# Delta attention with two FFNs: merge products with fp32 operands, the split of T once behind them

## The chip, the cores and the metric

The kernel runs on one core of one Trainium2 chip. The metric is the device time of one execution in microseconds, as the median of several runs. A core has a matrix engine (TensorE, PE in the profile; its weight loads are PEld), a vector engine (VectorE, DVE), a scalar engine (ScalarE, ACT), GpSimd (POOL) and SyncE (SP), which issues the DMAs. They work from the on-chip memory SBUF; TensorE writes its sums to PSUM, from where VectorE and ScalarE fetch them.

## What is computed

A linear attention with the delta rule over 4 batches x 8 heads, 768 positions, head size 48, and on its output two feed-forward networks one after the other (3072 tokens, width 384, hidden 2048). All data are fp32.

```python
k_n = k / (np.linalg.norm(k, axis=-1, keepdims=True) + 1e-06)
for t in range(S):
    y[:, :, t] = np.einsum('bhd,bhde->bhe', q[:, :, t], state)
    v_old = np.einsum('bhde,bhd->bhe', state, kt)
    state = state + bt[:, :, :, None] * np.einsum('bhd,bhe->bhde', kt, vt - v_old)
x = y.transpose(0, 2, 1, 3).reshape(B * S, H * D)
h = x @ w1_in;  x = np.maximum(0.01 * h, h) @ w1_out
h = x @ w2_in;  out = (h - np.tanh(h)) @ w2_out
```

## The kernel before

**Attention in chunks.** The 768 positions are cut into 12 chunks of 64 (n = 0 to 11), two of them to a pair u = 0 to 5. In a chunk the recurrence is replaced by products with a triangular 64x64 matrix T per head: the inverse of one plus the lower triangle of the scaled key gram. A pair has MM = 32 such matrices (2 chunks x NM = 16, with two heads on the upper and lower 64 partitions).

**How T is made.** `grams(n)` multiplies the keys with each other. `g_batch` (line 1035) writes the two diagonal 32x32 blocks of each gram to the room `gd` and the block below the diagonal, split, to `AT`. `inverses(u)` (line 1074) inverts the 32x32 blocks on VectorE, 58 small operations for j = 1 to 30 on all matrices at once, scales the result X, splits it into two fp16 halves Xh, and transposes them once into `nat` (natural order) and once into the second half of `XF`. `merges(u, nat)` (line 1097) then makes the off-diagonal block of T, which is minus one inverse times AT times the other, in two rounds of 32x32 products: the first makes `PM`, the second the block, which goes to `XF`. For u in `M8` (2 to 5) `merges8` does the same with the tiles laid so that eight places of the array are used. `states(n)` multiplies T by the corrected values and keeps the running state; `queries`, `products`, `outputs` make the chunk's output, a tile x of 256 tokens; `to_xa` scales, splits and turns it for the first FFN.

**Precision.** A product of two fp32 operands is made of fp16 ones: each operand is split into a high and a low half (`split`: ScalarE writes the rounded half, VectorE the remainder), and `heads` issues the three products high*high, high*low, low*high into the same sum. A split costs one ScalarE and one VectorE operation.

**FFN.** A token group n has two layers, (n,0) and (n,1), in the order (0,0), (1,0), (0,1), (1,1), (2,0) and so on. A layer has eight steps `h_part` and `o_part`, of groups of 9 or 6 matmuls with full 128x128 weights. The weights are loaded, read from 64-bit words, scaled and split at the start by VectorE and ScalarE (`weight`).

**Rooms.** Tiles come from rings with a number of rooms: `x` (XROOMS; FFN inputs, staging of weights and first keys, at most AMOST = 3 attention outputs at a time), `sx` (SROOMS; scratch), `gd` (one room), `xi` (one room, X).

**What sets the order.** The program is written down as a graph of nodes. `schedule` lays all nodes out with a cost model and one clock per engine: at each point it gives an engine the ready node with the least priority value, which is minus its remaining chain minus an offset from the table `BIAS`, by the node's stage. The resulting order is issued as it is. An operation given with two engines (`cp`) goes to the one that is free. TensorE's small products and FFN groups are issued in turn; `SMALL` holds the cost of one small product by tiling (`quad`), `PAGE` the time that 128 instructions take at least. All matmuls are issued at line 604 and all other operations at line 607, so the profile tells them apart by their tiles.

Of the kernel before, what the change touches and what calls it, by code (L numbers as in the profile page):

```python
# [48 lines left out]
SROOMS = 5  # L49
# [4 lines left out]
    ('consts', 0): -13.87, ('dma', 'b', 0): -307.84, ('dma', 'b', 1): 178.64, ('dma', 'grams', 10): 31.26,  # L54
    ('dma', 'grams', 11): 81.2, ('dma', 'grams', 2): -3.33, ('dma', 'grams', 3): 206.92,
    ('dma', 'grams', 4): 173.01, ('dma', 'grams', 5): 291.69, ('dma', 'grams', 6): 82.58,
    ('dma', 'grams', 7): -8.85, ('dma', 'grams', 8): 154.73, ('dma', 'grams', 9): 159.8,
    ('dma', 'k', 0): 160.49, ('dma', 'k', 1): 57.69, ('dma', 'keys', 10): -43.44, ('dma', 'keys', 11): 40.67,
# [9 lines left out]
    ('dma', 'products', 6): 125.73, ('dma', 'products', 7): -28.88, ('dma', 'products', 8): -7.04,
    ('dma', 'products', 9): 30.32, ('dma', 'queries', 0): 172.91, ('dma', 'queries', 1): 115.5,
    ('dma', 'queries', 10): 41.1, ('dma', 'queries', 11): 122.18, ('dma', 'queries', 2): 73.07,  # L70
    ('dma', 'queries', 3): -96.38, ('dma', 'queries', 4): 119.05, ('dma', 'queries', 5): 26.55,
    ('dma', 'queries', 6): 136.8, ('dma', 'queries', 7): 111.64, ('dma', 'queries', 8): 154.85,
    ('dma', 'queries', 9): 14.63, ('dma', 'to_xa', 1, 1): 130.41, ('dma', 'to_xa', 10, 1): -18.33,
    ('dma', 'to_xa', 11, 1): 29.42, ('dma', 'to_xa', 2, 1): 176.19, ('dma', 'to_xa', 3, 1): -89.32,
    ('dma', 'to_xa', 4, 1): 449.54, ('dma', 'to_xa', 5, 1): 14.05, ('dma', 'to_xa', 6, 1): 131.82,
    ('dma', 'to_xa', 7, 1): 86.81, ('dma', 'to_xa', 8, 1): 25.93, ('dma', 'to_xa', 9, 1): 128.46,
    ('dma', 'v', 0): 204.26, ('dma', 'weight', 0, 0): 102.51, ('dma', 'weight', 0, 1): 117.67,
    ('dma', 'weight', 0, 2): 0.89, ('dma', 'weight', 0, 3): 158.58, ('dma', 'weight', 0, 4): 46.07,
    ('dma', 'weight', 0, 5): -45.97, ('dma', 'weight', 1, 0): 67.45, ('dma', 'weight', 1, 1): 81.55,
    ('dma', 'weight', 1, 2): 53.58, ('dma', 'weight', 1, 3): 102.01, ('dma', 'weight', 1, 4): -5.39,  # L80
    ('dma', 'weight', 1, 5): 203.98, ('dma', 'weight', 2, 0): 114.99, ('dma', 'weight', 2, 1): 178.09,
    ('dma', 'weight', 2, 2): 127.03, ('dma', 'weight', 2, 3): 174.42, ('dma', 'weight', 2, 4): -73.56,
    ('dma', 'weight', 2, 5): 35.14, ('dma', 'weight', 3, 0): 125.81, ('dma', 'weight', 3, 1): 37.25,
    ('dma', 'weight', 3, 2): 113.91, ('dma', 'weight', 3, 3): 83.78, ('dma', 'weight', 3, 4): 355.28,
    ('dma', 'weight', 3, 5): 297.75, ('first_keys', 0): -39.35, ('grams', 0): 40.8, ('grams', 0, 1): 22.94,
    ('grams', 1): 38.75, ('grams', 1, 1): -39.7, ('grams', 10, 1): 144.33, ('grams', 11, 1): -20.86,
    ('grams', 2, 1): 51.08, ('grams', 3, 1): -75.12, ('grams', 4, 1): 7.24, ('grams', 5, 1): -0.11,
    ('grams', 6, 1): 173.8, ('grams', 7, 1): 4.91, ('grams', 8, 1): 56.4, ('grams', 9, 1): 20.21,
# [7 lines left out]
    ('inverses', 2, 1): -24.61, ('inverses', 3): -36.01, ('inverses', 3, 1): 11.53, ('inverses', 4): -32.07,
    ('inverses', 4, 1): 105.6, ('inverses', 5): 257.21, ('inverses', 5, 1): -51.28, ('keys', 10): -0.31,
    ('keys', 11): -76.39, ('keys', 2): 38.41, ('keys', 3): -12.4, ('keys', 4): -4.68, ('keys', 5): -349.49,
    ('keys', 6): 50.02, ('keys', 7): -41.11, ('keys', 8): 56.89, ('keys', 9): -8.53, ('merges', 0): 66.31,
    ('merges', 2): 165.98, ('merges', 3): 90.69, ('merges', 4): 190.95, ('merges', 5): 51.66,  # L100
# [6 lines left out]
    ('outputs', 10, 1): 37.88, ('outputs', 11, 1): 38.21, ('outputs', 2, 1): 2.77, ('outputs', 3, 1): 93.97,  # L107
    ('outputs', 4, 1): 141.64, ('outputs', 5, 1): -19.0, ('outputs', 6, 1): 8.74, ('outputs', 7, 1): 128.81,
    ('outputs', 8, 1): 206.17, ('outputs', 9, 1): 5.82, ('products', 0): 23.33, ('products', 1): 19.0,
    ('products', 10): 133.22, ('products', 11): 15.61, ('products', 2): 189.16, ('products', 3): 165.45,  # L110
    ('products', 4): -13.34, ('products', 5): -8.58, ('products', 6): -3.82, ('products', 7): -1.91,
    ('products', 8): 29.1, ('products', 9): -10.35, ('queries', 0): 287.56, ('queries', 1): -40.81,
    ('queries', 10): -12.87, ('queries', 11): 81.5, ('queries', 2): 13.89, ('queries', 3): -13.13,
    ('queries', 4): 153.28, ('queries', 5): -16.43, ('queries', 6): 35.77, ('queries', 7): 157.84,
    ('queries', 8): 9.36, ('queries', 9): 55.72, ('states', 0): -10.01, ('states', 0, 1): 0.39,
    ('states', 0, 2): -161.78, ('states', 1): 73.59, ('states', 1, 1): 17.21, ('states', 1, 2): 21.55,
    ('states', 10): -7.11, ('states', 10, 1): 9.72, ('states', 10, 2): 6.87, ('states', 11): -174.19,
    ('states', 11, 1): -16.97, ('states', 2): -23.01, ('states', 2, 1): 118.94, ('states', 2, 2): -9.83,
    ('states', 3): 31.95, ('states', 3, 1): -7.84, ('states', 3, 2): 17.01, ('states', 4): 37.67,
    ('states', 4, 1): 104.03, ('states', 4, 2): -34.7, ('states', 5): 76.0, ('states', 5, 1): 119.15,  # L120
    ('states', 5, 2): -13.08, ('states', 6): 8.7, ('states', 6, 1): 80.62, ('states', 6, 2): 83.82,
# [1449 lines left out]
```

## Time and profile before

| | us |
|---|---|
| median of 3 runs (990.19 to 990.79) | 990.56 |
| profiled execution | 990.11 |
| its span in the trace | 988.4 |
| TensorE busy | 875.9 (89%) |
| VectorE busy | 723.5 (73%) |
| ScalarE busy | 594.7 (60%) |

Busy shares are means over stages with different limits, so they are read by stages: first in the 40 slices of the page, then in the table of stretches. Matmuls overlap in the array: the duration of one is longer than the distance to the next, and a group's cost is read from the start of one group to the start of the next. The granted TensorE clock is 0.999 of full speed over the span.

### The profile page before, as it was taken

How to read it: one execution, taken by the hardware profiler on the slowest of the kernel's cores; microseconds unless marked ns; L12 is line 12 of the kernel's file. 1: busy time of each engine (PE TensorE's matmuls, PEld its weight loads, DVE VectorE, ACT ScalarE, POOL GpSimd, SP SyncE). 2: the span in 40 equal slices, each digit the busy share in tenths (PEclk: the TensorE clock that was granted, in tenths of full speed). 3: DMA queues.
4: the chain of work that ended last, by engine and by line, in shares of the span. 5: the costliest groups of instructions: out<-in, count | busy, mean ns of one | idle time of the engine just before them, and what ended most of it. 6: DMA issues, size and time to landing. Idle time of an engine off the chain costs nothing.

```text
span 988.4 us, 37304 instructions
## 1 busy us (share of the span) xinstructions
PE 875.9 (89%) x16680; PEld 719.4 (73%) x16680; DVE 723.5 (73%) x1714; ACT 594.7 (60%) x1324; POOL 5.9 (1%) x21
## 2 busy tenths in 40 slices
PE   1102399999999999999999999999999999999997
PEld 1102378887788887788877788887788878788875
DVE  7999999999799764699576896764479647342432
ACT  6949865777886864476866545852554545434431
POOL 2000000000000000000000000000000000000000
PEclk9999999999999999999999999999999999999999
DMA  9952544320524000331002300110110001010000
GB/s 354 398 161 65 164 150 135 112 83 26 125 78 93 4 18 18 60 92 43 19 19 62 77 19 19 46 40 18 38 31 18 3 1 40 18 35 1 2 17 17
DMA packets 69280, 67.11 MB, mean 68 GB/s; under 512 B 42752, under 2 KB 54016, under 8 KB 69120
## 3 DMA queue, kind: packets, MB, share of 16 engines
q1 hardware_dynamic: 69120, 64.74, 23.3%
q8 instruction: 130, 2.13, 0.9%
q14 instruction: 30, 0.25, 0.1%
HBM read 44.14 MB, written 4.72 MB: 49 GB/s over the span
## 4 chain that ended last, share of the span: by engine, by line
PE 73%; DVE 13%; ACT 8%; DMA 3%; issue 2%; SPq 0%; ACTq 0%; DVEq 0%
PE ps_h L604 34%; PE ps_o L604 32%; PE ps_a L604 7%; ACT sx L607 2%; DVE wi L607 2%; ACT jk L607 2%; DVE xi L607 2%; DVE wo L607 2%; DVE sx L607 2%; ACT XF L607 1%; DMA kf<-in_k_dram 1%; DVE gd L607 1%; DVE g L607 1%; DVE pq L607 1%; ACT gd L607 1%
## 5 line engine op out<-in xcount | busy, mean ns | idle before, releaser
L604 PE MATMUL ps_h<-x,wi 128*128 128x256 f16 x3456 | 408.9, 274 | 0.8 <-DVE sx L607 0.5
L604 PEld LDWEIGHTS <-wi 128*128 128x128 f16 x3456 | 334.7, 98 | 49.4 <-issue 2.6
L604 PE MATMUL ps_o<-g,wo 128*128 128x256 f16 x1728 | 204.8, 273 | 0.1
L604 PE MATMUL ps_o<-wo,g 128*128 128x384 f16 x1152 | 200.7, 326 | 0.4 <-ACT sx L607 0.4
L604 PEld LDWEIGHTS <-wo 128*128 128x128 f16 x1728 | 166.7, 98 | 19.6
L607 ACT ACTIVATE g<-sx 128x512 f16<-128x512 f32 x192 | 120.3, 627 | 90.4 <-DVE sx L607 51.7
L604 PEld LDWEIGHTS <-g 128*128 128x128 f16 x1152 | 110.7, 98 | 66.8 <-issue 0.9
L607 DVE SCALAR_TENSOR_TENSOR sx<-sx,kap,ps_h 128x512 f32<-128x512 f32 x96 | 71.4, 744 | 65.3 <-ACT sx L607 65.1
L607 ACT ACTIVATE sx<-ps_h,kap 128x512 f32<-128x512 f32 x96 | 65.1, 679 | 65.7 <-PE ps_h L604 50.8
L607 DVE TENSOR_TENSOR g<-sx,g 128x512 f16<-128x512 f32 x96 | 65.8, 686 | 47.0 <-ACT g L607 46.4
L607 DVE SCALAR_TENSOR_TENSOR g<-sx,g 128x512 f16<-128x512 f32 x96 | 66.2, 689 | 45.7 <-ACT g L607 45.4
L607 ACT ACTIVATE sx<-ps_h 128x512 f32<-128x512 f32 x96 | 56.9, 592 | 68.9 <-PE ps_h L604 48.6
L607 DVE TENSOR_TENSOR gd<-xi 128x30 f32<-128x30 f32 (+9 forms) x180 | 58.8, 327 | 2.2
L607 DVE TENSOR_TENSOR xi<-xi,gd 128x30 f32<-128x30 f32 (+9 forms) x180 | 59.0, 328 | 2.0
L604 PEld LDWEIGHTS <-ones 128*128 128x128 bf16 x124 | 8.0, 100 | 59.3 <-issue 45.1
L604 PEld LDWEIGHTS <-KTp 48*64 48x64 f16 x3360 | 34.3, 114 | 19.9 <-issue 19.3
L607 ACT ACTIVATE jk<-kf 128x48 bf16<-128x48 f32 x160 | 38.4, 240 | 4.3 <-DMA kf<-in_k_dram 0.9
L604 PE MATMUL ps_a<-ab,ones 128*128 128x1 bf16 x60 | 7.9, 166 | 29.4 <-ACT sx L607 23.8
L607 ACT ACTIVATE sx<-x 128x768 bf16<-128x768 f32 x24 | 20.2, 843 | 20.0 <-DVE x L607 19.6
L607 DVE SCALAR_TENSOR_TENSOR XF<-ps_a,XF 32x256 f16<-32x256 f32 (+1 forms) x40 | 19.9, 497 | 15.2 <-ACT XF L607 14.2
L607 ACT ACTIVATION_READ_ACCUMULATOR jk<-kf 128x1 f32 x160 | 30.1, 188 | 0.0
L607 DVE SCALAR_TENSOR_TENSOR wi<-wo,wi 128x768 int32<-128x768 int32 x32 | 29.7, 948 | 0.0
(138 smaller groups left out, 983.0 us busy)
## 6 DMA issues: line engine op xcount, KB each, us to landing
wo<-in_w_in_dram SPq DMA_DIRECT2D x32, 384.0 KB, 7.9
qf<-in_q_dram SPq DMA_DIRECT2D x24, 256.0 KB, 2.9
wi<-in_w_out_dram SPq DMA_DIRECT2D x14, 384.0 KB, 8.0
kf<-in_k_dram SPq DMA_DIRECT2D x12, 384.0 KB, 4.1
vf<-in_v_dram SPq DMA_DIRECT2D x12, 384.0 KB, 3.5
out_dram<-sx SPq DMA_DIRECT2D x48, 96.0 KB, 2.2
x<-in_w_out_dram SPq DMA_DIRECT2D x10, 384.0 KB, 5.6
b<-in_beta_dram SPq DMA_DIRECT2D x6, 512.0 KB, 4.0
```

The source lines that it names most:

```text
L604: self.eng["pe"].matmul(out=o.real(), lhsT=lhsT.real(), rhs=rhs.real(), start=start, stop=stop)
L607: getattr(self.eng[n.on], op)(**{k: v.real() if isinstance(v, View) else v for k, v in kw.items()})
```

## The change

The 32x32 products of both merge rounds take fp32 operands: one product in place of three fp16 ones. What they read is no longer split: `AT` and `PM` are fp32 tiles, each written by one copy, and the inverse's result is transposed as fp32. The transposed X in natural order goes to the room of `gd` and not to that of X. T is split at the end of `merges`, once per chunk of the pair: ScalarE copies to a new tile `XH`, and VectorE writes the remainder to `XF`. `states` reads the high half from `XH`. `gd` has two rooms, `x` four in place of six, `sx` six in place of five. The two forms of the merge are one function. The planner counts an fp32 product as two instructions and has two more costs in `SMALL`. All offsets in `BIAS` have other values.

```diff
-XROOMS = 6
+XROOMS = 4
...
-SROOMS = 5
+SROOMS = 6
...
-    SMALL = ((0.0163, 0.028), (0.0094, 0.0139), (0.0065, 0.0139))
+    SMALL = ((0.0163, 0.028), (0.0094, 0.0139), (0.0065, 0.0139), (0.027, 0.045), (0.017, 0.03))
...
+        node.cnt += 1 + (lhsT.ap.dtype == F32)
...
-    gd_r = ring("gd", 1, MM * HB)
+    gd_r = ring("gd", 2, MM * HB)
...
-    AT = fixed("AT", [128, 2, NM, 2 * HB], F16)
-    PM = fixed("PM", [128, 2, NM, HB], F16)
+    AT = fixed("AT", [128, NM, 2 * HB], F32)
+    PM = fixed("PM", [128, NM, HB], F32)
     XF = fixed("XF", [128, MM, C, 2], F16)
+    XH = fixed("XH", [128, MM, C], F16)
...
-            split(AT[:, 0, av], AT[:, 1, av], ps.rearrange("p (m a) n -> p m (a n)", a=2)[:, :, HB:HB + C], 1.0 / KS)
+            cp(AT[:, av], ps.rearrange("p (m a) n -> p m (a n)", a=2)[:, :, HB:HB + C], 1.0 / KS)
...
-        Xh = Gd.rearrange("p m j -> p (m j)").bitcast(F16).rearrange("p (i j c) -> p i j c", i=HB, c=2)
-        nat = X.rearrange("p m j -> p (m j)").bitcast(F16).rearrange("p (m j c) -> p m j c", m=MM, c=2)
-        copy(Xh[:, :, :, 0], X)
-        tt(Xh[:, :, :, 1], X, Xh[:, :, :, 0], ALU.subtract)
-        transpose(packed(nat).rearrange("p m j -> p j m"), packed(Xh).rearrange("p i j -> p j i"))
-        transpose(XW[:, :, HB:].rearrange("p m i -> p i m"), packed(Xh))
+        nat = Gd
+        transpose(nat.rearrange("p m j -> p j m"), X.rearrange("p i j -> p j i"))
+        transpose(XW[:, :, HB:].rearrange("p m i -> p i m"), X)
...
+        def rounds(jobs):
+            ps = banks(HB)
+            for m in range(GM):
+                for f, h in HF:
+                    jobs(ps[f], m, m + f * GM, HQ[2 * h], HQ[2 * h + 1], *spots(f, h))
+            return ps
+
+        def first(ps, m, i, up, dn, out_up, out_dn):
+            mm(ps[out_dn, m], AT[up, i, 0:HB], nat[up, 2 * i])
+            mm(ps[out_up, m], AT[dn, i, HB:], tt_[dn, 2 * i + 1])
+
+        def second(ps, m, i, up, dn, out_up, out_dn):
+            mm(ps[out_up, m], PM[dn, i], tt_[dn, 2 * i])
+            mm(ps[out_dn, m], nat[up, 2 * i + 1], PM[up, i])
+
+        ps = rounds(first)
+        for f in range(2):
+            fm = slice(f * GM, (f + 1) * GM)
+            if f and eight:
+                for h in range(2):
+                    cp(PM[HS[h], fm], ps[f][HS[1 - h]], 1.0 / KS)
+            else:
+                cp(PM[:, fm], ps[f], 1.0 / KS)
+        ps = rounds(second)
...
+                    cp(xm[HQ[2 * h], a][:, f * GM:(f + 1) * GM], ps[f][spots(f, h)[a]], -1.0 / KS)
+        for s in range(2):
+            g_.stage = "merges", u, s
+            ms = slice(s * NM, (s + 1) * NM)
+            copy(XH[:, ms], XW[:, ms])
+            tt(XF[:, ms, :, 0], XW[:, ms], XH[:, ms], ALU.subtract)
...
-                heads([(ps[g][HS[h ^ g], m], [XF[HS[h], m0 + g * GM + m, :, c_] for c_ in range(2)],
+                heads([(ps[g][HS[h ^ g], m], [XH[HS[h], m0 + g * GM + m], XF[HS[h], m0 + g * GM + m, :, 0]],
```

## Rows read from the trace of the kernel before

**Rows 1.** The page: shares by engine, and TensorE's busy tenths in 40 slices

```profile
PE 875.9 (89%) x16680; PEld 719.4 (73%) x16680; DVE 723.5 (73%) x1714; ACT 594.7 (60%) x1324; POOL 5.9 (1%) x21
...
PE   1102399999999999999999999999999999999997
```

**Rows 2.** Table by stages: stretch, length, busy us of PE, PEld, DVE, ACT, POOL

```profile
0.00:100.00 100.00, 14.70 (x905) 12.81 (x906) 92.66 (x236) 72.81 (x239) 5.87 (x21) 1.00 0.69 244
100.00:125.00 25.00, 8.63 (x444) 7.87 (x428) 24.07 (x38) 21.43 (x41) 0.00 (x0) 1.00 0.58 168
...
200.00:250.00 50.00, 50.00 (x1125) 39.50 (x1123) 49.13 (x109) 37.43 (x62) 0.00 (x0) 1.00 0.21 63
250.00:300.00 50.00, 49.49 (x1290) 38.58 (x1279) 44.95 (x130) 40.50 (x127) 0.00 (x0) 1.00 0.42 101
...
950.00:988.00 38.00, 33.27 (x253) 24.41 (x250) 12.31 (x18) 11.15 (x18) 0.00 (x0) 0.99 0.09 22
```

**Rows 3.** Order of time, TensorE: start us, duration us, instruction group, count

```profile
245.97 1.15 PE L604 MATMUL ps_h<-x,wi 128*128 128x256 f16 x9
246.96 1.14 PE L604 MATMUL ps_o<-wo,g 128*128 128x384 f16 x6
```

**Rows 4.** Order of time, TensorE, around one merge round

```profile
478.33 2.13 PE L604 MATMUL ps_h<-x,wi 128*128 128x256 f16 x18
480.38 0.18 PE L604 MATMUL ps_a<-XF,PM 32*32 32x32 f16 x1
...
481.92 0.18 PE L604 MATMUL ps_a<-PM,xi 32*32 32x32 f16 x1
482.04 2.69 PE L604 MATMUL ps_o<-g,wo 128*128 128x256 f16 x23
```

**Rows 5.** Table by stages, only instructions on PM: TensorE, weight loads, VectorE, ScalarE

```profile
85.00:130.00 45.00, 1.90 (x192) 1.67 (x96) 0.69 (x1) 0.57 (x1) 1.00 0.44 134
...
465.00:485.00 20.00, 1.72 (x192) 1.59 (x96) 1.27 (x3) 1.14 (x3) 1.00 0.10 32
```

**Rows 6.** Costliest groups by form, VectorE, then ScalarE: count, busy us, mean ns

```profile
L607 DVE SCALAR_TENSOR_TENSOR XF<-ps_a,XF 32x256 f16<-32x256 f32 x32 | 14.1, 440 | 14.5 <-ACT XF L607 13.7
...
L607 DVE SCALAR_TENSOR_TENSOR AT<-ps_a,AT 128x256 f16<-128x256 f32 x24 | 9.9, 417 | 0.3 <-ACT AT L607 0.2
...
L607 DVE TENSOR_TENSOR gd<-xi,gd 128x1024 f16<-128x1024 f32 x6 | 8.2, 1360 | 2.1 <-ACT gd L607 2.0
...
L607 DVE SCALAR_TENSOR_TENSOR XF<-ps_a,XF 32x512 f16<-32x512 f32 x8 | 5.8, 722 | 0.7 <-ACT XF L607 0.6
...
L607 ACT ACTIVATE XF<-ps_a 32x256 f16<-32x256 f32 x32 | 14.4, 449 | 10.2 <-PE ps_a L604 8.0 <-DVE XF L607 1.4
...
L607 ACT ACTIVATE AT<-ps_a 128x256 f16<-128x256 f32 x24 | 8.7, 382 | 1.3 <-DVE gd L607 1.2
L607 ACT ACTIVATE gd<-xi 128x1024 f16<-128x1024 f32 x6 | 8.1, 1348 | 1.7 <-DVE xi L607 1.7
...
L607 ACT ACTIVATE PM<-ps_a 128x256 f16<-128x256 f32 x4 | 1.5, 384 | 0.1
```

**Rows 7.** Order of time, VectorE and ScalarE, around the first merge

```profile
80.74 0.19 DVE L607 TENSOR_SCALAR xi<-b 128x32 f32<-128x32 f32 x1
...
84.83 2.06 DVE L607 STREAM_TRANSPOSE xi<-gd 128x1024 f32<-128x1024 f32 x1
...
103.10 0.71 ACT L607 ACTIVATE XF<-ps_a 32x512 f16<-32x512 f32 x1
...
110.42 0.73 DVE L607 SCALAR_TENSOR_TENSOR XF<-ps_a,XF 32x512 f16<-32x512 f32 x1
```

**Rows 8.** Order of time, TensorE: the first FFN group

```profile
129.13 5.33 PE L604 MATMUL ps_h<-x,wi 128*128 128x256 f16 x27
```

**Rows 9.** Order of time: the third group's turning DMAs, and its first FFN products

```profile
267.58 3.06 SPq L607 DMA_TRANSPOSE x<-sx  x2
...
274.42 1.16 PE L604 MATMUL ps_h<-x,wi 128*128 128x256 f16 x9
```

More of the change, by code (lines that the diff above doesn't have):

```diff
@@ L53 @@
 BIAS = {
[L54 to L58, printed above, removed]
@@ L68 @@
[L68 to L73, printed above, removed]
@@ L74 @@
[L74 to L88, printed above, removed]
[6 rows of a table removed]
-    ('inverses', 0, 1): 133.5, ('inverses', 1): -36.38, ('inverses', 1, 1): 15.22, ('inverses', 2): 14.02,
@@ L96 @@
[L96 to L100, printed above, removed]
[6 rows of a table removed]
@@ L107 @@
[L107 to L121, printed above, removed]
@@ L137 @@
-    ('weight', 2, 3): 129.61, ('weight', 2, 4): -141.25, ('weight', 2, 5): -344.98, ('weight', 3): 225.17,
-    ('weight', 3, 0): -12.03, ('weight', 3, 1): -38.44, ('weight', 3, 2): 187.06, ('weight', 3, 3): -214.7,
-    ('weight', 3, 4): -52.05, ('weight', 3, 5): -64.53,
+    ('consts', 0): 44.43, ('dma', 'b', 0): -17.81, ('dma', 'b', 1): -51.45, ('dma', 'grams', 10): -22.99,
+    ('dma', 'grams', 11): -129.47, ('dma', 'grams', 2): -0.05, ('dma', 'grams', 3): 125.77,
+    ('dma', 'grams', 4): -19.78, ('dma', 'grams', 5): 12.19, ('dma', 'grams', 6): 1.87,
@@ new lines @@
+    ('dma', 'grams', 7): 35.25, ('dma', 'grams', 8): 31.51, ('dma', 'grams', 9): -132.02,
+    ('dma', 'k', 0): 296.83, ('dma', 'k', 1): 143.48, ('dma', 'keys', 10): -31.98, ('dma', 'keys', 11): -101.3,
+    ('dma', 'keys', 2): -110.92, ('dma', 'keys', 3): 52.43, ('dma', 'keys', 4): -15.95,
+    ('dma', 'keys', 5): -130.9, ('dma', 'keys', 6): 92.75, ('dma', 'keys', 7): -8.09, ('dma', 'keys', 8): 1.78,
+    ('dma', 'keys', 9): 8.74, ('dma', 'o_part1', 0): -21.77, ('dma', 'o_part1', 1): 2.63,
[3 rows of a table added]
+    ('dma', 'o_part1', 9): 0.54, ('dma', 'products', 1): -1.65, ('dma', 'products', 10): -65.54,
@@ new lines @@
+    ('dma', 'products', 11): -88.37, ('dma', 'products', 2): 27.28, ('dma', 'products', 3): 18.26,
+    ('dma', 'products', 4): -65.22, ('dma', 'products', 5): 40.06, ('dma', 'products', 6): 64.27,
+    ('dma', 'products', 7): -62.2, ('dma', 'products', 8): -4.58, ('dma', 'products', 9): -255.86,
+    ('dma', 'queries', 0): 84.04, ('dma', 'queries', 1): -7.71, ('dma', 'queries', 10): -17.82,
+    ('dma', 'queries', 11): -69.89, ('dma', 'queries', 2): -186.5, ('dma', 'queries', 3): 3.67,
+    ('dma', 'queries', 4): -29.26, ('dma', 'queries', 5): 34.02, ('dma', 'queries', 6): 174.44,
@@ new lines @@
+    ('dma', 'queries', 7): -27.52, ('dma', 'queries', 8): -38.4, ('dma', 'queries', 9): -6.15,
+    ('dma', 'to_xa', 1, 1): -42.59, ('dma', 'to_xa', 10, 1): 22.52, ('dma', 'to_xa', 11, 1): 48.23,
+    ('dma', 'to_xa', 2, 1): 26.16, ('dma', 'to_xa', 3, 1): -478.07, ('dma', 'to_xa', 4, 1): 1.83,
+    ('dma', 'to_xa', 5, 1): 237.5, ('dma', 'to_xa', 6, 1): 35.5, ('dma', 'to_xa', 7, 1): -16.95,
+    ('dma', 'to_xa', 8, 1): 51.23, ('dma', 'to_xa', 9, 1): 3.9, ('dma', 'v', 0): 225.47,
+    ('dma', 'weight', 0, 0): -27.26, ('dma', 'weight', 0, 1): -156.01, ('dma', 'weight', 0, 2): -11.99,
@@ new lines @@
+    ('dma', 'weight', 0, 3): 1.29, ('dma', 'weight', 0, 4): -89.97, ('dma', 'weight', 0, 5): -86.75,
+    ('dma', 'weight', 1, 0): -23.46, ('dma', 'weight', 1, 1): 5.49, ('dma', 'weight', 1, 2): 50.54,
+    ('dma', 'weight', 1, 3): 10.62, ('dma', 'weight', 1, 4): -20.79, ('dma', 'weight', 1, 5): -31.76,
+    ('dma', 'weight', 2, 0): -56.23, ('dma', 'weight', 2, 1): 143.18, ('dma', 'weight', 2, 2): 8.17,
+    ('dma', 'weight', 2, 3): 214.07, ('dma', 'weight', 2, 4): -20.18, ('dma', 'weight', 2, 5): 226.33,
@@ new lines @@
+    ('dma', 'weight', 3, 0): 128.96, ('dma', 'weight', 3, 1): 187.1, ('dma', 'weight', 3, 2): -31.75,
+    ('dma', 'weight', 3, 3): -26.07, ('dma', 'weight', 3, 4): 51.88, ('dma', 'weight', 3, 5): -38.04,
+    ('first_keys', 0): 57.64, ('grams', 0): -24.9, ('grams', 0, 1): 125.6, ('grams', 1): 115.12,
+    ('grams', 1, 1): 1.43, ('grams', 10, 1): -13.77, ('grams', 11, 1): 22.01, ('grams', 2, 1): 108.23,
+    ('grams', 3, 1): 39.17, ('grams', 4, 1): 5.07, ('grams', 5, 1): 5.39, ('grams', 6, 1): 11.59,
@@ new lines @@
+    ('grams', 7, 1): 51.09, ('grams', 8, 1): 374.08, ('grams', 9, 1): 184.06, ('h_part0', 1): -13.01,
[5 rows of a table added]
+    ('h_part1', 9): 90.06, ('inverses', 0): 273.98, ('inverses', 0, 1): 131.38, ('inverses', 1): -6.39,
+    ('inverses', 1, 1): -109.27, ('inverses', 2): -211.61, ('inverses', 2, 1): -3.41, ('inverses', 3): -28.95,
+    ('inverses', 3, 1): -5.18, ('inverses', 4): 3.56, ('inverses', 4, 1): -104.28, ('inverses', 5): -95.8,
+    ('inverses', 5, 1): 102.63, ('keys', 10): 61.37, ('keys', 11): 23.57, ('keys', 2): 122.59,
@@ new lines @@
+    ('keys', 3): -6.83, ('keys', 4): -11.38, ('keys', 5): -13.92, ('keys', 7): 24.96, ('keys', 8): -37.52,
+    ('keys', 9): -120.64, ('merges', 0, 0): 126.87, ('merges', 0, 1): -43.4, ('merges', 1): 5.6,
+    ('merges', 1, 0): 1.89, ('merges', 1, 1): -51.37, ('merges', 2): 39.99, ('merges', 2, 0): 20.13,
+    ('merges', 2, 1): 23.04, ('merges', 3): 784.36, ('merges', 3, 0): 2.83, ('merges', 3, 1): 47.44,
+    ('merges', 4): 26.05, ('merges', 4, 0): 0.64, ('merges', 4, 1): 18.95, ('merges', 5): 17.46,
[7 rows of a table added]
@@ new lines @@
+    ('outputs', 10, 1): 20.55, ('outputs', 11, 1): 59.41, ('outputs', 2, 1): 66.82, ('outputs', 3, 1): 345.83,
+    ('outputs', 4, 1): 183.51, ('outputs', 5, 1): 2.83, ('outputs', 6, 1): 33.99, ('outputs', 7, 1): 47.99,
+    ('outputs', 8, 1): -13.85, ('outputs', 9, 1): -39.8, ('products', 0): 125.94, ('products', 1): 28.97,
+    ('products', 10): 21.01, ('products', 11): -64.74, ('products', 2): -90.46, ('products', 3): -17.53,
+    ('products', 4): 117.48, ('products', 5): -18.97, ('products', 6): 202.39, ('products', 7): 5.4,
@@ new lines @@
+    ('products', 8): -29.14, ('products', 9): -56.63, ('queries', 0): -6.34, ('queries', 1): 172.78,
+    ('queries', 10): 3.07, ('queries', 11): -21.08, ('queries', 2): -7.18, ('queries', 3): 139.78,
+    ('queries', 4): -38.97, ('queries', 5): -5.89, ('queries', 6): 77.76, ('queries', 7): 7.73,
+    ('queries', 8): 11.86, ('queries', 9): -130.03, ('states', 0): 117.73, ('states', 0, 1): 1.16,
+    ('states', 0, 2): 118.21, ('states', 1): 29.8, ('states', 1, 1): 127.32, ('states', 1, 2): 222.14,
@@ new lines @@
+    ('states', 10): 85.47, ('states', 10, 1): -38.5, ('states', 10, 2): 0.5, ('states', 11): 2.26,
+    ('states', 11, 1): 47.85, ('states', 2): 21.61, ('states', 2, 1): 275.33, ('states', 2, 2): -13.21,
+    ('states', 3): -63.86, ('states', 3, 1): 59.1, ('states', 3, 2): -80.7, ('states', 4): -30.61,
+    ('states', 4, 1): 24.82, ('states', 4, 2): 261.68, ('states', 5): 91.41, ('states', 5, 1): -3.9,
+    ('states', 5, 2): -118.03, ('states', 6): 6.89, ('states', 6, 1): 109.91, ('states', 6, 2): 12.47,
@@ new lines @@
+    ('states', 7): 28.51, ('states', 7, 1): 4.1, ('states', 7, 2): -1.55, ('states', 8): 129.07,
+    ('states', 8, 1): 96.12, ('states', 8, 2): -5.11, ('states', 9): 0.64, ('states', 9, 1): 136.26,
+    ('states', 9, 2): -103.01, ('to_xa', 0): 63.34, ('to_xa', 0, 1): 73.9, ('to_xa', 1): 14.69,
+    ('to_xa', 10): 9.0, ('to_xa', 2): 40.2, ('to_xa', 3): -15.21, ('to_xa', 4): -3.44, ('to_xa', 5): 82.58,
+    ('to_xa', 6): 95.59, ('to_xa', 7): 45.37, ('to_xa', 8): -3.58, ('to_xa', 9): -1.28, ('to_xb', 0): 29.67,
@@ new lines @@
+    ('v_scale', 9): 11.54, ('weight', 0): 8.04, ('weight', 0, 0): 5.8, ('weight', 0, 1): 245.24,
+    ('weight', 0, 2): 60.75, ('weight', 0, 3): -2.78, ('weight', 0, 4): 49.61, ('weight', 0, 5): 5.35,
+    ('weight', 1): 60.34, ('weight', 1, 0): 2.29, ('weight', 1, 1): 277.75, ('weight', 1, 2): 16.46,
+    ('weight', 1, 3): 38.15, ('weight', 1, 4): -13.11, ('weight', 1, 5): 52.14, ('weight', 2): 155.89,
+    ('weight', 2, 0): -61.34, ('weight', 2, 1): 12.16, ('weight', 2, 2): -6.18, ('weight', 2, 3): 86.59,
@@ L140 @@
+    ('weight', 2, 4): 201.91, ('weight', 2, 5): 9.67, ('weight', 3): -4.9, ('weight', 3, 0): 234.55,
+    ('weight', 3, 1): 127.64, ('weight', 3, 2): 37.63, ('weight', 3, 3): 0.46, ('weight', 3, 4): 7.5,
+    ('weight', 3, 5): -39.32,
 }
@@ L345, in matmul @@
             self.open.warm = self.open.cold = 0.0
-            self.open.mode = 0
+            self.open.mode = self.open.cnt = 0
             self.open.stage = self.stage
@@ L511, in schedule @@
             if e == "pe" and n.mode:
[L512 removed]
+                c = n.cnt
                 at = t + (n.warm * left_on / c if c >= left_on else n.warm + (left_on - c) * 0.109)
@@ L1098, in merges @@
         g_.stage = "merges", u
-        def two(t, r, m):
-            return [t[r, m, :, c_] for c_ in range(2)]
-        tt_ = XF[:, :, HB:]
-        def bank2():
-            t = g_.tile(ps_a, [128, 512], F32)
-            g_.cut()
-            return t.rearrange("p (m n) -> p m n", m=NM)
-        xm = tt_.rearrange("p (m a) i c -> p a m i c", a=2)
-        if u in M8:
-            merges8(u, nat, two, tt_, xm)
-            return
-        ps = bank2()
-        for m in range(NM):
-            if m == GM:
-                g_.cut()
-            jobs = []
-            for h in range(2):
-                up, dn = HQ[2 * h], HQ[2 * h + 1]
-                jobs += [(ps[dn, m], [AT[up, c_, m, 0:HB] for c_ in range(2)], two(nat, up, 2 * m)),
-                         (ps[up, m], [AT[dn, c_, m, HB:] for c_ in range(2)], two(tt_, dn, 2 * m + 1))]
-            heads(jobs)
@@ L1124, in merges @@
-        split(PM[:, 0], PM[:, 1], ps, 1.0 / KS)
-        ps = bank2()
-        for m in range(NM):
-            if m == GM:
-                g_.cut()
-            jobs = []
-            for h in range(2):
-                up, dn = HQ[2 * h], HQ[2 * h + 1]
-                jobs += [(ps[up, m], parts(PM, dn, m), two(tt_, dn, 2 * m)),
-                         (ps[dn, m], two(nat, up, 2 * m + 1), parts(PM, up, m))]
-            heads(jobs)
-        for a in range(2):
-            for h in range(2):
-                o = xm[HQ[2 * h], a]
-                split(o[:, :, :, 0], o[:, :, :, 1], ps[HQ[2 * h + a]], -1.0 / KS)
@@ new lines, in merges, with spots @@
+        tt_ = XW[:, :, HB:]
+        eight = u in M8
+        HF = [(f, h) for f in range(2) for h in range(2)]
+        g_.quad = 4 if eight else 3
+        def spots(f, h):
+            w = h ^ f if eight else h
+            return HQ[2 * w], HQ[2 * w + 1]
+        def rounds(jobs):
[7 more added lines that the diff above has]
+            mm(ps[out_up, m], AT[dn, i, HB:], tt_[dn, 2 * i + 1])
@@ L1167, in merges8 @@
         g_.quad = True
+        xm = tt_.rearrange("p (m a) i -> p a m i", a=2)
         for f in range(2):
@@ L1247, in states @@
                 for m in range(GM):
-                    heads([(ps[HS[h], m], [XF[HS[h], m0 + g * GM + m, :, c_] for c_ in range(2)],
+                    heads([(ps[HS[h], m], [XH[HS[h], m0 + g * GM + m], XF[HS[h], m0 + g * GM + m, :, 0]],
                             parts(R[:, g], HS[h], m)) for h in range(2)])
```

60 lines of the change are left out of this document (8 added, 52 removed), and 30 rows, old and new, of the table BIAS.

## The prediction, on record before the changed kernel was run

> **What bounds the kernel now.** I read the page's shares first, then the table by stages, then the order of time on TensorE. TensorE is busy 89% of a span of 988.4 us, and its slices show why it is not more: four slices almost empty, then nines to the end [rows 1]. By stages [rows 2] the first 100 us hold 14.70 us of TensorE work, while VectorE is busy 92.66; in 100 to 125 VectorE has 24.07 of 25. From there TensorE is the full one: 50.00 of 50 in 200 to 250, 49.49 in 250 to 300. The last stretch, 33.27 of 38, holds the final scaling and store. The FFN begins at 129.13 [rows 8]. So the time is a start of 129 us that VectorE and one chain set, and after it a TensorE that goes from one FFN group to the next, with the attention's small products put between them. What the change takes off TensorE after 129 us comes off the time one for one, as long as each FFN layer finds its input. What it takes off VectorE counts only up to the first layers: VectorE is still busy 49.13 of 50 in 200 to 250 and 44.95 in the next 50 [rows 2], and the input of the third token group is turned by DMAs issued at 267.58 and first used at 274.42 [rows 9]. The run-up to that use is nearly as tight as the start.
>
> **The price of a small product.** A merge of one chunk pair u has two rounds of 192 products with 32x32 operands in fp16 [rows 5]. The order of time shows a whole round: it begins at 480.38, its last product starts at 481.92 and the FFN goes on at 482.04 [rows 4]. That is 1.66 us, of which 1.54 go to 191 steps: 8.1 ns per product, and some 0.12 us for leaving the mode. An FFN group of nine products with 256 columns takes 0.99 us from its start to the next group's [rows 3], 110 ns per product or 0.43 ns per column; 32 columns at that rate are 13.8 ns. So the small products already overlap in the array, and what I see is a rate of instructions. After the start there are five merges, ten rounds, at 1.66 us: 16.6 us.
>
> **Part 1: fp32 products instead of three fp16 ones.** 64 products per round take the place of 192. No row shows an fp32 product. The diff counts each as two instructions, and that decides my value: two at the measured rate of 8.1 ns are 16.2 ns, 64 of them 1.04 us, with entering and leaving 1.2 us. The low end is one instruction's price: 64 x 8.1 ns + 0.12 = 0.64 us. The high end is an fp32 product that goes through four times and overlaps with none: 4 x 13.8 = 55 ns, a round of 3.5 us. I take 1.2, because the operands and output tiles lie in the same places as in the overlapping rounds. Ten rounds then give 12.0 instead of 16.6 us: **-4.6 us**, with ends -10 and +19.
>
> The Trainium skill (FP8 and Floating Point Precision, "TensorE Precision Notes") says that a true fp32 product takes four passes through the array. No run here shows one. By four passes at the instruction price a round is 64 x 4 x 8.1 ns = 2.07, with 0.12 it is 2.2 us: ten rounds cost 22, or 5.3 us more than now. It stands below as a rival.
>
> **Part 2: the start.** For the first merge the steps lie on the chain to the first FFN product.
> - The inverse's last step is at 80.74, done at 80.93; the transposes begin at 84.83 [rows 7]. In between lies the split of X that the change deletes: 1.36 us on ScalarE and 1.33 on VectorE here, with weight work between. The transposes read X itself now. Gain up to 3.9 us; if weight work fills the place, only VectorE's own 1.3.
> - The first round's result was split in 0.57 + 0.69 us, one behind the other [rows 5]. Now two halves are copied, 0.38 each [rows 6], on either engine at once: -0.7 to -0.9.
> - The second round's result was split from 103.10 to 111.15 (110.42 + 0.73) [rows 7], 8.0 us, of which four pairs with 0.72 each are 5.8 [rows 6]. Now eight copies at 0.44 to 0.45 over two engines are 1.8 us, and then come the copy to XH and the subtraction for the first half, 1024 elements each, 1.35 and 1.36 by the rows of the old split with the same size [rows 6]: 4.5 us. With the 2.2 us of foreign work that lay between, 6.7: -1.3.
> - First and second round on TensorE: 64 against 192 products; at 1.2 for 1.66 us, -0.5 each at the same rate.
> Together -3.9 - 0.8 - 1.3 - 1.0 = -7.0 for the chain by itself. But VectorE was full in those stretches, and what is pulled forward pushes weight conversion back, which the second FFN layers need. VectorE's own account for the first two merges limits the gain: before, 1.36 + 0.69 + 4 x 0.72 + 4 x 0.42 (the split of AT) = 6.6 us each; after, two subtractions of 1.36 and a half of the fourteen copies (4 AT, 2 PM, 8 XF, together 5.9) = 5.7, or 2.7 if ScalarE, which has 72.8 of 100 us in use at the start [rows 2], takes them all. So VectorE is relieved by 1 to 4 us per merge, 2 to 8 over both. I take **-5 us** for the first FFN product, and the same for the third group's input. Ends: -8, and +3 if the two new steps at the end (2.7 us) stand on the chain while the place of the old split fills with other work.
>
> **Part 3: what moves without a price.** Later merges save more vector work (eight pairs of 0.44 become eight copies, the AT split halves), but no engine except TensorE is full after 300 us: nothing. The states' products read the upper part from XH and the lower from XF; same count, same shape: nothing. The second gram room lets the next chunk pair's grams be written while the inverse, which now keeps its result in that room, is still being read. Without it the next grams would wait for the second merge round; with it nothing waits. Two x rooms fewer: a token group's input and the second layer's input hold a room for one layer each, and three attention inputs at most are admitted as before, so four rooms hold a pair and the next pair; the two that staged weights are free again before the third group. If that is wrong the price shows at the third group, whose use follows the turning by only 274.42 - 267.58 = 6.8 us, most of it the DMAs. One more scratch room can only admit work earlier. New offsets put every step at another place; the single idle pieces in the stages after 150 are some tenths of a microsecond (0.51 in 250 to 300 [rows 2]), so an order as dense as this gains no more than 2 us, and a worse one may cost as much: 0, +-2.
>
> **Sum.** Against the profiled execution (990.11 us: span 988.4 and 1.7 around it): 990.1 - 4.6 - 5 = 980.5. The median of the runs, 990.56, is 0.45 above, so the prediction is **981 us**.
>
> **Rivals.**
> *The start gives its gain back.* VectorE was the full engine until 250 us; the FFN begins earlier, but the second weights or the third group's input come as late as before, and TensorE idles for the difference. For it: 49.13 of 50 in 200 to 250. Against it: VectorE loses work too. Then only Part 1 counts: 990.6 - 4.6 = 986.
> *Four times the price, by the rule above.* +5.3 on ten rounds, -5 from the start: about 991, no change. Against it: two instructions per product in the diff. For it: the row's rate was only seen with fp16.
> *fp32 products do not overlap (slower).* Place: the ten rounds after 129 us and the two before. Price: 3.5 + 0.12 against 1.66 us, +2.0 each, +20; the start's -5 becomes about -1 since its two rounds are longer by 4. Time: 990.6 + 20 - 1 = 1009. Break-even is where ten rounds cost 16.6 + 5 us: 2.16 us each, less 0.12, 32 ns per product. From there on it is slower. Against it: the fp16 rounds overlap with the same tiles.
>
> The Trainium skill (TensorEngine Tiling (Array Packing), "Instruction Overhead") gives each matmul an overhead of about 60 cycles, 25 ns at 2.4 GHz. The round of 192 in 1.66 us says 8.1 ns; as a rate the rule does not hold here. By it, 64 instructions fewer per round would be -16 us over ten rounds instead of -4.6, and I give it no weight.
>
> **How the numbers follow.** Chances: forecast 0.52, start given back 0.15, four times the price 0.13, no overlap 0.10, and 0.10 that the new order is worse than the old by more than it saves (a wait for a room or for the third group; 993 to 1000). Faster by over 0.2% (about what a measurement of this kernel can tell from no change, 2 us) are the first two: 0.67; within it 0.13; slower 0.20. The range leaves out 2 in 10, half of it at each end: below, merges at 0.8 us per round (-8.6) and a start of -8 give 974; above, it takes in the no-change case and the beginning of the worse orders: 995.
>
> **What would show it.** Right: TensorE's matmul records fall by 2304 fp16 and rise by 1536 (two per fp32 product); a round takes 1.1 to 1.3 us from its first product to the next FFN group; transposes start within 1 us of the inverse's last step; the first FFN product is at 124, the third group's input as much earlier. Wrong: rounds over 2.1 us, a first FFN product after 129, or TensorE idle in 150 to 300 that before was not there.

## The result

The changed kernel takes 978.86 us (median of four runs, 977.31 to 981.46) against 990.67 for the kernel before: a ratio of 0.9884, 95% interval 0.9863 to 0.9906. It is 1.2% faster, 11.8 us; the prediction said 981. The profiled execution took 978.71 us with a span of 977.0, 11.4 less than before.

The page of the changed kernel shows the same picture as [rows 1], with 768 matmul records fewer (15912 for 16680):

```profile
PE 872.3 (89%) x15912; PEld 716.6 (73%) x15912; DVE 700.9 (72%) x1653; ACT 584.2 (60%) x1329; POOL 5.9 (1%) x21
...
PE   2201499999999999999999999999999999999997
```

The stages of [rows 2] after the change (stretch, length, busy us of PE, PEld, DVE, ACT, POOL, then granted clock, DMA share, GB/s). VectorE is about as full as before up to 200 us (92.34 for 92.66 in the first 100) and a little less in 200 to 250 (46.87 for 49.13), where TensorE now stands 2.4 us:

```profile
0.00:100.00 100.00, 17.92 (x889) 15.28 (x893) 92.34 (x233) 66.20 (x180) 5.87 (x21) 1.00 0.69 238
100.00:125.00 25.00, 11.41 (x527) 10.07 (x520) 25.00 (x42) 20.95 (x44) 0.00 (x0) 1.00 0.62 174
...
200.00:250.00 50.00, 47.63 (x967) 36.97 (x965) 46.87 (x119) 35.08 (x66) 0.00 (x0) 1.00 0.28 67
250.00:300.00 50.00, 49.79 (x1193) 39.23 (x1192) 46.04 (x119) 37.29 (x119) 0.00 (x0) 1.00 0.36 87
```

A merge round in the order of time on TensorE, to be held against [rows 4], and one of the four groups of fp32 products:

```profile
333.98 0.21 PE L608 MATMUL ps_a<-XF,PM 32*32 32x32 f32 x1
...
335.07 0.19 PE L608 MATMUL ps_a<-PM,gd 32*32 32x32 f32 x1
335.20 0.50 PE L608 MATMUL ps_o<-g,wo 128*128 128x256 f16 x3
...
L608 PE MATMUL ps_a<-PM,gd 32*32 32x32 f32 x384 | 8.6, 205 | 0.0
```

The round takes 335.20 - 333.98 = 1.22 us. Four groups of 384 records are 1536 for 768 products: an fp32 product is two matmul records in the trace. The first FFN product, the third group's turning DMAs and its first products, against [rows 8, 9]:

```profile
124.53 3.41 PE L608 MATMUL ps_h<-x,wi 128*128 128x256 f16 x18
...
264.43 2.57 SPq L611 DMA_TRANSPOSE x<-sx  x2
...
270.40 3.11 PE L608 MATMUL ps_h<-x,wi 128*128 128x256 f16 x27
```

**Where the 11.4 us of the span went.** The FFN begins 4.6 us earlier (129.13 to 124.53). From there to the end it takes 852.5 in place of 859.3 us, 6.8 less. The ten rounds are 3.7 of that: nine of 1.22 and one of 2.04, in which TensorE stood, 0.6 us of it in one wait; 13.0 for 16.8. The other 3.0 us are spread: adding up from each matmul's start to the next one's, FFN products take 764.5 us for 767.0, the chunks' other small products 65.5 for 67.4 (one group of 96 moved ahead of the first FFN product), and the sums over partitions 4.0 for 2.7, with a wait of 1.4 for VectorE behind one of them, until 246.21.

### The profile page after: what moved, and what is told of

It reads as the page before. It is cut to its first block, busy times and chain, and to the rows that moved or that the text cites. A ratio compares the mean times of both kernels' runs of the same rounds, so it can differ in the third digit from the quotient of the medians.

```text
span 977.0 us, 35741 instructions
## 1 busy us (share of the span) xinstructions
PE 872.3 (89%) x15912; PEld 716.6 (73%) x15912; DVE 700.9 (72%) x1653; ACT 584.2 (60%) x1329; POOL 5.9 (1%) x21
## 4 chain that ended last, share of the span: by engine, by line
PE 83%; DVE 8%; DMA 4%; ACT 3%; issue 1%; SPq 1%; ACTq 0%; DVEq 0%
PE ps_o L608 38%; PE ps_h L608 37%; PE ps_a L608 8%; DVE wi L611 2%; DVE wo L611 2%; DMA wi<-in_w_out_dram 1%; ACT jk L611 1%; DMA wo<-in_w_in_dram 1%; DVE sx L611 1%; DMA kf<-in_k_dram 1%; DMA qf<-in_q_dram 1%; ACT sx L611 1%; DVE gd L611 1%; DVE XF L611 1%; SPq L611 1%
## 5 line engine op out<-in xcount | busy, mean ns | idle before, releaser
L608 PE MATMUL ps_h<-x,wi 128*128 128x256 f16 x3456 | 403.1, 273 | 2.3 <-DVE sx L611 1.7
L608 PE MATMUL ps_o<-g,wo 128*128 128x256 f16 x1728 | 200.0, 273 | 0.3 <-issue 0.2
L608 PE MATMUL ps_a<-wacc,ones 128*128 128x1 bf16 x64 | 2.7, 165 | 34.7 <-ACT wi L611 24.6
L611 DVE TENSOR_SCALAR p<-ps_a 128x1 f32<-128x1 f32 x40 | 6.2, 154 | 37.1 <-PE ps_a L608 37.0
L611 ACT ACTIVATE sx<-x,sxs 128x768 f16<-128x768 f32 (+1 forms) x26 | 22.8, 880 | 13.7 <-DVE sxs L611 13.6
```

Source lines behind the costliest of these rows:

```text
L608: self.eng["pe"].matmul(out=o.real(), lhsT=lhsT.real(), rhs=rhs.real(), start=start, stop=stop)
L611: getattr(self.eng[n.on], op)(**{k: v.real() if isinstance(v, View) else v for k, v in kw.items()})
```

## The experiments

All kernels run beside the kernel before. In six of them the planner's order of the changed kernel is kept: an edit is made where the order is issued, and the planner does not know of it. Their base is the changed kernel once more, on the chip of the first three (each fp32 product twice, three 16-bit products, the split at the first pair). The other three (one and two 16-bit products, the split at the pairs 2 to 5) ran on another chip, on which the kernel before took 990.30 us for 990.72; there the ratio to the kernel before is compared too.

**The base.** 

> The changed kernel, unaltered, on the chip on which the three next kernels run, as their base. Both theories: 977 to 981.5 us, as in its four runs so far (median 978.86).

It took 979.26 us (978.90 to 979.65), a ratio of 0.9886.

**Each fp32 product twice.**

```diff
-                    self.eng["pe"].matmul(out=o.real(), lhsT=lhsT.real(), rhs=rhs.real(), start=start, stop=stop)
+                    for _ in range(1 + (lhsT.ap.dtype == F32)):
+                        self.eng["pe"].matmul(out=o.real(), lhsT=lhsT.real(), rhs=rhs.real(), start=start, stop=stop)
```

> The changed kernel in its own order, but every fp32 merge product is issued twice, the second writing the same sum again: 768 products more. It prices the fp32 product by itself. Theory (the array is the full engine after the start, so a product's price comes on the time one for one): a round of 64 takes 1.22 us in the trace of the changed kernel, less some 0.14 for changing the mode 1.08, so ten rounds after the start cost 10.8 us more, and the two on the start chain up to 2 more: 990 to 992. Rival (the merges lie in time that the array had free, and the gain came from the order): at most 3 us more, 982.

Measured: 1034.61 us, 55 more than the base and five times what the theory said. Neither side had it.

**Three 16-bit products in place of one fp32.** The array work of the kernel before, in the new order.

```diff
+                    a, b, times = lhsT.real(), rhs.real(), 1
+                    if lhsT.ap.dtype == F32:
+                        a, b = (x.bitcast(BF16)[:, 1::2] for x in (a, b))
+                        times = 3
+                    for _ in range(times):
+                        self.eng["pe"].matmul(out=o.real(), lhsT=a, rhs=b, start=start, stop=stop)
```

> The changed kernel in its own order, but each fp32 merge product is replaced by three 16-bit ones (the upper halves of the same words, read as bf16, each writing the sum anew, so the off-diagonal blocks of T have 16-bit precision only): 192 products a round as before the change. It undoes the first part alone. Theory: 192 at 8.1 ns and 0.12 are 1.66 us against 1.22, so ten rounds cost 4.4 us more and the two in the start up to 0.9: 983 to 984. Rival (the number of products does not matter): 977 to 981, as the base.

Measured: 1003.73 us, 24.5 more; neither side had that. The first round of each later pair takes 1.72 us, near the 1.66 expected, but the second, some 4 to 6 us later, takes 2.1 to 4.4. Of the 24.9 us between the two profiled spans, 13.8 lie in the ten rounds, 6.3 in the FFN products, 3.2 ahead of the first FFN product (127.96 for 124.74) and 1.6 in the rest. What TensorE waited for (us in total, times, longest), first the changed kernel, then this one, then the one with each product twice:

```profile
PE ps_a L608 <- issue: 7.7, 4, 2.9
```

```profile
PE ps_a L613 <- issue: 20.2, 12, 2.9
```

```profile
PE ps_a L609 <- issue: 32.5, 19, 2.9
```

"Issue" is a wait for nothing that the profile shows. One second round, and, from the table of stretches in the run with three products, a stretch behind the long wait of each of the first four later pairs (the clock stands after POOL's busy time):

```profile
347.67 0.19 PE L613 MATMUL ps_a<-PM,gd 32*32 32x32 bf16 x1 [1.76 <-issue]
...
250.00:259.00 9.00, 7.09 (x95) 4.52 (x95) 5.78 (x11) 5.76 (x13) 0.00 (x0) 0.50 0.31 59
349.00:352.00 3.00, 3.00 (x16) 2.07 (x15) 2.56 (x14) 2.90 (x7) 0.00 (x0) 0.50 0.01 3
472.00:474.00 2.00, 2.00 (x11) 1.45 (x10) 0.00 (x0) 1.91 (x6) 0.00 (x0) 0.50 0.00 0
633.00:643.00 10.00, 9.96 (x141) 8.96 (x141) 4.19 (x5) 6.75 (x13) 0.00 (x0) 1.00 0.01 3
```

TensorE stood 1.76 us in the middle of a round. Behind three of the four long waits (2.21 us until 248.31, 1.76 until 347.67, 1.87 until 470.09) the granted clock fell for a while to 0.50, the lower of its two levels (1.2 of 2.4 GHz); behind the fourth (1.87 until 633.04) it stayed at 1.00, as it does in the base from 130 to 970 us. So many small instructions in a short time cost a wait, and mostly clock in the FFN behind it.

What the wait is for shows in a count of the matmul records. In every kernel of this case the page counts one packet on the DMA queue "instruction" for 128.3 matmul records (16680 for 130, 15912 for 124, 17448 for 136). The traces of all thirteen kernels hold 87 "issue" waits of TensorE longer than 0.4 us. In each trace they end a multiple of 128 records after the first of them, to within 4 records in some 16000, and each of the 87 ends 0.8 to 1.6 us after a packet of that queue has landed. No two of these packets start less than 3.29 us apart. So TensorE waited for the next block of instructions. Two rounds of 192 records are three such blocks; in the four pairs with a long wait the second round began 3.8 to 4.8 us behind the first, in the fifth, which waited 0.2 us, 6.1 us. The Trainium skill (Runtime: NRT & Kernel Launch, "Instruction fetch mechanics") says that the instruction memory is refilled in blocks and that crossing a boundary is mostly hidden; in these bursts it was not. The kernel before has no such wait in its ten later rounds: four of them are cut in two with 3.05 us of FFN products between, and a fifth with 7.0 us of FFN and other products. The edit added products to an order that was not made for them, so the 24.5 us are not what three products cost in an order of their own.

**One and two 16-bit products** in place of each fp32 one, the same edit with `times` 1 and 2. Against the changed kernel, the first halves the merge records and the second leaves their number as it is.

> The changed kernel in its own order, but each fp32 merge product is replaced by one 16-bit product (the upper halves of the same words, read as bf16, so the off-diagonal blocks of T have 16-bit precision only): 64 instructions a round in place of 128. Three products in place of one added 24 us, because from the second round on TensorE stood for its instructions; with fewer instructions that cannot happen, so this run prices the product alone. Theory (price times count): a round goes from 1.22 to 64 x 8.1 ns + 0.12 = 0.64 us, ten rounds give 5.8 us back: 973 to 974 against 979.3 for the base. Rival (the products cost nothing as long as instructions keep up, and the gain came from that): 978 to 980.

> The same with two 16-bit products in place of each fp32 one: the count of instructions that the diff assumes for fp32, 128 a round, without fp32. Theory (an fp32 product costs what two instructions cost): a round of 1.16 to 1.22 us, the time within 1 us of the base, 978.5 to 980. Rival (the fp32 passes cost by themselves, beyond the instructions): a round under 0.9 us, 975 to 976.

One product: 976.22 us, 3.0 less than the base (2.6 by the ratios, 0.9860 for 0.9886); the rounds take 0.58, so ten of them came 6.6 us lower, and less than half of that came off the time. Most of the rest went where the theory had not looked:

```profile
240.00:250.00 10.00, 6.92 (x103) 4.55 (x100) 8.72 (x21) 8.06 (x18) 0.00 (x0) 0.83 0.59 115
```

Ahead of the third group TensorE stands 3 of 10 us: its wait for ScalarE grew from 0.4 us in the base to 1.8, while one of 1.3 for VectorE is in the base too (1.4). The granted clock is 0.83 over these 10 us and 1.00 in the base, and the third group begins 1.9 us later than there (272.19 for 270.31). Two products: 978.12 us (ratio 0.9879) with rounds of 1.15, 0.07 under fp32, as the theory said. So an fp32 product costs nearly what its two instructions cost, and the products do count, though not one for one.

**The old split of the inverse put back at the first pair**, results unused, one ScalarE and one VectorE operation ahead of the transposes:

```diff
+        if u in (0,):
+            Xh = Gd.rearrange("p m j -> p (m j)").bitcast(F16).rearrange("p (i j c) -> p i j c", i=HB, c=2)
+            node.ahead = [("act", "activation", dict(out=Xh[:, :, :, 0], in_=X, func=ACTF.Copy, scale=1.0)),
+                          ("dve", "tensor_tensor", dict(out=Xh[:, :, :, 1], in0=X, in1=Xh[:, :, :, 0], op=ALU.subtract))]
```

> The changed kernel in its own order, with the old split of the first pair's inverse put back ahead of its transposes, results unused: one ScalarE copy (1.36 us) and one VectorE subtraction (1.33 us) one after the other, for u = 0 only. Theory (the chain of the first merge sets the first FFN product, and that the end): the chain grows by 2.7 to 3 us, the first FFN product moves from 124.5 to some 127, the end by as much: 981 to 982. Rival (an earlier start is given back before the third group): the first FFN product moves and the end does not: within 1 us of the base.

Measured: 981.68 us (979.91 to 982.34), 2.4 more, which is in the theory's range. But the first FFN product moved only from 124.74 in the base to

```profile
126.22 3.46 PE L609 MATMUL ps_h<-x,wi 128*128 128x256 f16 x18
```

by 1.5 us and not by 2.7. In the profiled run the shift is 1.0 us at 191 us, 2.0 at the third group, behind a stretch (248.3 to 251.7) in which the granted clock was 0.50 and in the base 1.00, and 3.1 at the end. So the end does move, against the rival; but part of the shift was absorbed on the way and more came from the clock and from small pieces after 500 us. That a microsecond of the start is a microsecond of the end is not shown.

**The same at the pairs 2 to 5**, meant as the control:

> The control of e3_split_first: the old split of the inverse's result put back, unused, for the pairs u = 2 to 5 and not for the first. Four times 2.7 us of ScalarE and VectorE work, but after 300 us. Theory (the split counted at the start only, where the chain sets the first FFN product): within 1 us of the base, 978.5 to 980.3. Rival (VectorE's load counts everywhere): 4 x 1.4 to 4 x 2.7 us more, 985 to 990.

Measured: 985.90 us, 6.6 more (by the ratios too, 0.9953 for 0.9886). The theory was wrong and the rival right. VectorE in one such place, then TensorE there (order of time):

```profile
324.33 1.36 DVE L612 TENSOR_TENSOR gd<-xi,gd 128x1024 f16<-128x1024 f32 x1 [1.49 <-ACT gd L612]
325.73 2.10 DVE L614 STREAM_TRANSPOSE gd<-xi 128x1024 f32<-128x1024 f32 x1
327.70 1.92 DVE L614 STREAM_TRANSPOSE XF<-xi 128x1024 f32<-128x1024 f32 x1
329.48 1.25 DVE L614 TENSOR_TENSOR g<-sx,g 128x512 f16<-128x512 f32 x2
...
329.20 0.27 PE L609 MATMUL ps_o<-g,wo 128*128 128x256 f16 x1
330.20 2.02 PE L609 MATMUL ps_o<-g,wo 128*128 128x256 f16 x17 [0.73 <-DVE g L614]
```

VectorE takes its operations in the order in which they were issued. It waits 1.49 us for ScalarE, subtracts for 1.36, and then come two transposes of 2 us each; the FFN's own step (g) starts at 329.48, in the base at 325.79 (0.9 us of that was already there when the inverse ended), and TensorE runs out of FFN work. Between FFN products one step took 0.9 us too long here, and 1.7, 1.9 and 1.1 us at the other three inverses. VectorE is not full there (70.84 of 100 us in 300 to 400 in the changed kernel); what counts is how long it is away at a stretch. The run does not say what the old split cost there in the old order, where other work stood between; in the accounting above nothing of that size stands out, as the spread part is 3.0 us in all.

**Rooms alone.** The kernel before with XROOMS 4 and two gram rooms.

> The kernel before with four x rooms and two gram rooms, nothing else. The planner issues the same order of instructions with it as without, so no step waits for one of these rooms. Theory: the time of the kernel before, 990 to 991.5. Rival (two gram rooms let the next pair start earlier, or four x rooms hold a group back): off by more than 2 us.

Measured: 990.55 us, ratio 1.0002 (0.9993 to 1.0012). TensorE, VectorE and ScalarE run the same operations in the same order as without. So these rooms do nothing by themselves in the kernel before. The sixth room of `sx` was not tried alone, nor was the changed kernel with one gram room.

**The offsets.** Three runs: the offsets of the kernel before searched further, those of the changed kernel searched further, and the changed kernel with those of the kernel before.

> The kernel before with nothing changed but the offsets, which a search of 8400 steps with the planner's own layout moved from where they were. It asks whether new offsets alone could have made the gain. Theory (the gain is in the products and the chain): within 1.5 us of before, 988.5 to 991.5. Rival (the kernel before only had bad offsets): 980 to 985.

> The changed kernel with its offsets moved by the same search, of 8600 steps. Theory: no more than the spread of the changed kernel, 977 to 980.5. Rival (the changed kernel's offsets left as much lying as the change brought): below 975.

> The changed kernel with all offsets of the kernel before; the new stages of the split of T have none. It does the change without its new order. Theory (offsets belong to the steps that they were made for; with others the order leaves TensorE waiting): slower than the changed kernel by over 5 us, 985 to 1005, with the first FFN product or the third group's input late. Rival (the gain is in the steps, whatever the order): 978 to 983.

The kernel before: 989.77 us, ratio 0.9992 (0.9982 to 1.0001). The search that far found nothing clear of noise in it, as the theory said. The changed kernel: 975.79 us, ratio 0.9852 (0.9837 to 0.9866), 3 us below the change itself: a smaller gain than the rival said, a larger one than the theory allowed. Its first FFN product comes earlier again:

```profile
122.32 3.92 PE L854 MATMUL ps_h<-x,wi 128*128 128x256 f16 x17
```

The changed kernel with the old offsets: 994.61 us, slower than before by 0.5% (ratio 1.0047, 1.0032 to 1.0062) and within the theory's range:

```profile
130.09 1.85 PE L605 MATMUL ps_h<-x,wi 128*128 128x256 f16 x9
...
264.96 1.07 PE L605 MATMUL ps_a<-SP,KTp 48*64 48x48 f16 x96 [1.69 <-DVE x L608]
...
281.75 1.15 PE L605 MATMUL ps_h<-x,wi 128*128 128x256 f16 x9
...
250.00:300.00 50.00, 45.36 (x1057) 34.75 (x1055) 41.11 (x107) 34.99 (x116) 0.00 (x0) 1.00 0.57 111
```

The FFN begins 1 us later than before, the third group 7 us later, and TensorE stands 4.6 us in 250 to 300. The steps alone bring no gain if the order was made for others.

## Why the prediction was right, and where its steps were not

**The frame held.** The FFN's begin, the third group's input and TensorE's work behind them set the time. First FFN product 124 predicted, 124.53 measured; third group 5 us earlier predicted, 4.0 measured; 0.6 of the 4.6 us at the start had gone by then.

**Part 1 held in its price.** 1.2 us per round predicted, 1.22 measured; -4.6 us predicted, -3.7 measured, as one round took 0.8 us longer: it began 3.3 us behind the first round of its pair and waited for instructions. Two 16-bit products in the same places take 1.15, so the mechanism, two instructions' price, held too. Two of the rivals fall with it: at four times the price a round would be 2.2 us, without overlap 3.6. What I had missed is how the price turns into time. Instructions added in the fixed order cost far more than their own duration (24.5 and 55 us), as TensorE then waits for blocks of instructions, and products removed below the changed kernel's number gave back less than half (2.6 to 3.0 of 6.6 us).

**Part 2 had the right sum from wrong terms.** The first inverse and its merge after the change, against [rows 7] (VectorE, ScalarE, VectorE):

```profile
85.40 0.13 DVE L611 TENSOR_SCALAR xi<-b 128x32 f32<-128x32 f32 x1
...
85.99 1.99 DVE L611 STREAM_TRANSPOSE gd<-xi 128x1024 f32<-128x1024 f32 x1
...
94.97 2.60 ACT L611 ACTIVATE XF<-ps_a 32x256 f32<-32x256 f32 x8
97.60 2.00 ACT L611 ACTIVATE XH<-XF 128x1024 f16<-128x1024 f32 x2
...
101.04 1.29 DVE L611 TENSOR_TENSOR XF<-XF,XH 128x1024 f16<-128x1024 f32 x1
```

The inverse ends at 85.53, 4.6 us *later* than before (80.93): VectorE did other work first. From there to the first FFN product it is 39.0 us in place of 48.2, 9.2 less. The gap ahead of the transposes went from 3.9 to 0.5 us, as predicted. From the transposes' start to the first copy of the second round it went from 18.3 to 9.0 us, where I had counted 1.8 (two rounds and the copies of PM): this was the largest term. The prediction took 0.5 us off each round, as if only the price of a product counted. But in the kernel before TensorE waited three times for instructions in and between these two rounds, 5.9 us together:

```profile
92.23 0.18 PE L604 MATMUL ps_a<-XF,AT 32*32 32x32 f16 x1 [1.95 <-issue]
...
95.69 0.33 PE L604 MATMUL ps_a<-wacc,ones 128*128 128x1 bf16 x7 [1.34 <-issue]
...
99.69 0.18 PE L604 MATMUL ps_a<-PM,xi 32*32 32x32 f16 x1 [2.58 <-issue]
```

In the changed kernel, with 128 records a round, it did not wait so there. The run with three 16-bit products had two such waits there (2.09 and 2.80 us), and its first FFN product came 3.2 us later; so a good part of the earlier start comes from fewer instructions, and not from a shorter chain of splits alone. How the rest of the 9.3 us divides between the deleted splits and the foreign work that moved away, no run separates. From that copy to the end of the first half's split it is 7.4 for 8.0, half of the 1.3 predicted: the eight copies took only 2.60 us, all on ScalarE, but VectorE converted weights until 101.04 before it subtracted. From there on the chain took longer than before, 22.2 us to the first FFN product in place of 18.0. What the chain by itself gained, 9.2 us, was larger than my 7; what VectorE took back, 4.6, was larger than my 2; and that their difference is near my 5 is luck.

**The rival of the given-back start** fell by the trace itself, as 4.0 of the 4.6 us are still there at the third group, and by the split put back at the first pair: with the first FFN product 1.5 us later the end came 2.4 us later.

**Part 3 was wrong in two places.** The later vector work was set at nothing because VectorE is not full there. That reason does not hold: four insertions of 2.7 us cost 6.6 us in the fixed order. What the removed work had cost in the old order stays open. And the order itself was set at 0 +- 2: the part that is neither start nor rounds is -3.0 us, the search took another 3 off the changed kernel, and the old offsets cost it 15. One sign that I had named for a wrong prediction did show, TensorE idle for 2.4 us in 200 to 250; it is already inside the accounting above (0.6 in a round, 1.8 in the rest). Which of the new placements makes the 3.0 us was not tested. The rooms were right as far as they were tried: nothing. (In the listing `g_batch` begins at line 1029 and `inverses` at 1064; the text ahead of it gives 1035 and 1074.)

## What to carry to other kernels

Where one engine is full and the order is written out, ask of a change first what it does to the chain up to the first full stretch, then what it takes off the full engine. Here the second came out as sized from the trace, the first only in its sum. Count the instructions of a burst too: in the first merge 192 records a round in place of 128 meant waits that the price of one product does not show. A change of steps and the order that fits them belong together: with the old offsets this gain of 1.2% was a loss of 0.5%. And idle share is not room: an engine that works in order may be half idle and still stop another one, when it is away for longer than the other's stock of work lasts.

## What the runs showed of the hardware

An fp32 product of 32x32 operands is two matmul records. From a round's first record to its last, 127 steps, it is 1.10 us with fp32 and 1.05 with two 16-bit products (8.6 and 8.3 ns a step): 17.3 ns for an fp32 product, 16.5 for two 16-bit ones. Being fp32 costs almost nothing beyond the two instructions at this size.

TensorE's instructions come in blocks of 128 matmul records, and no two packets of the queue "instruction" start less than 3.29 us apart in these runs. A burst of 192 records in 1.72 us ran through; the next 192, begun 3.8 to 4.8 us behind the first, had a wait of 1.8 to 2.2 us in four of five pairs, and begun 6.1 us behind it one of 0.2. Behind three of these four waits the granted clock was 0.50 (1.2 GHz) for some 3 to 10 us. A wait of 2 us in the array can cost more than 2 us.
